# K and V loads in pairs of heads with 16 KB pieces, in a one-token decode kernel

**Chip and metric.** One core of one Trainium2 chip. The metric is the device time of the core in microseconds (us). Most executions agree within 0.3%.

**Words.** PE is the matmul engine and PEld its weight load; DVE, ACT and POOL are the vector, scalar and GpSimd engines; SP issues the loads (SPq is its queue). A *piece* is one contiguous run of bytes that a load brings to one partition. A *tick* is the count that one DMA engine adds to the load's semaphore when its share has landed: the trace holds 16 for each of these loads, with their times, though no view prints them. The *landing* of a load is its last tick.

## The reference, cut to what matters

One token `x` (512 wide) is normalised; an attention branch with 32 query heads over 8 K/V heads reads the last 4096 positions of two caches, and a gated MLP branch is added.

```python
W  = 4096                                     # min(4096, max(256, Sk // 4)), Sk = 65536
q  = (x @ wq).reshape(B, 1, 32, 128)          # wq: 512 x 4096
k, v = caches[:, :, Sk - W:, :]               # 8 heads x 4096 x 128, bf16, repeated 4 times
p  = softmax(q @ k.T * 128 ** -0.5)
a  = (p @ v).reshape(B, 1, 4096) @ wo         # wo: 4096 x 512
m  = (silu(x @ w_gate) * (x @ w_up)) @ w_down # 512 x 1792 twice, 1792 x 512
out = x_in + a + x + sigmoid(x @ w_r) * m     # x here is the normalised row
```

All weights and the used part of the caches are read once: 30.67 MB.

## The kernel before

SP issues all large loads in one order. Every load covers 128 partitions; with 16 DMA engines, each engine moves 8 partitions' pieces per load. For K and V a load is one head (1 MB), and a partition gets 32 consecutive positions, that is one piece of 8 KB.

```python
t_wq = [dma(sy, f"wq{h}", wq_sb[:, h * KH:(h + 1) * KH, :], wq_v[:, h * KH:(h + 1) * KH, :]) for h in range(2)]
t_k = [dma(sy, f"k{g}", k_sb[:, g].rearrange("p b (i d) -> p (b i) d", d=DH),
           A_k_cache[0, g, Sk - W:, :].rearrange("(p t) d -> p t d", t=NT)) for g in range(HKV)]
...                                            # then v0..v7, gate, up, wo in 4 chunks, w_down in 5
def T(b, i):                                   # 8 transposes of K on PE, into PSUM
    te.wait_ge(s_c[b], i)
    for k in range(8):
        ins = te.transpose(tp[:, b, k * P:(k + 1) * P], kin[:, b, k * P:(k + 1) * P], ident_bf[:])
    ins.then_inc(pe_t, 1)
def Sm(b, i, q, last=False):                   # 2 score matmuls, each on a column group of 32
    te.wait_ge(s_ev[b], i)
    for e in range(2):
        c = 2 * b + e
        cq, ch = c % 4, c // 4
        ins = te.matmul(sc[32 * cq:32 * cq + 32, ch, :], lhsT=q[:], rhs=kT[:, b, e * 512:(e + 1) * 512],
                        start=False, stop=False, tile_position=(0, 32 * cq), skip_group_check=True)
...
with te.Fori(1, 9) as i:                       # one head per turn, in two half steps
    T(0, i); T(1, i); te.wait_ge(s_qb, i); Sm(2, i, qB); Sm(3, i, qB, last=True)
    T(2, i); T(3, i); te.wait_ge(s_qa, i); Sm(0, i, qA); Sm(1, i, qA, last=True)
...                                            # softmax, P transposed, PV, then:
fill(F4)                                       # 2 * F4 filler matmuls
for k, (j0, j1) in enumerate(wo_chunks):       # 4 x 8 matmuls, each chunk waits for its load
    PE.need(t_wo[k]); ...
for k, (j0, j1) in enumerate(wd_chunks):       # 14 matmuls behind 5 loads
    PE.need(t_wd[k]); ...
```

Of the kernel before, what the change touches and what calls it, by code (L numbers as in the profile page):

```python
# [9 lines left out]
ALU = mybir.AluOpType  # L10
# [28 lines left out]
def kernel(  # L39
# [35 lines left out]
    W3, F1, F2, F3, F4 = 2, 2, 1, 2, 2  # L75

    sb = lambda name, shape, dt: nc.alloc_sbuf_tensor(name, shape, dt)
    k_sb = sb("k_sb", [P, HKV, 4, 1024], BF16)
    v_sb = sb("v_sb", [P, HKV, NT, DH], BF16)
    wq_sb = sb("wq_sb", [P, KT, NQ], BF16)  # L80
    kin = sb("kin", [P, 4, 1024], BF16)
    kT = sb("kT", [P, 4, 1024], BF16)
    p_sb = sb("p_sb", [P, 1024], BF16)
    vin = sb("vin", [P, 2, 16, DH], BF16)
    pTcur = sb("pTcur", [P, 8, 16], BF16)
    pvS = sb("pvS", [P, 4, DH], BF16)
    qpad = sb("qpad", [P, HKV, 32], BF16)
    qA = sb("qA", [P, 32], BF16)
    qB = sb("qB", [P, 32], BF16)
# [5 lines left out]
    ident_bf = sb("ident_bf", [P, P], BF16)  # L95
    ident_f = sb("ident_f", [P, P], F32)
# [4 lines left out]
    r32 = sb("r32", [P, 32], BF16)  # L101
    eps_t = sb("eps_t", [P, 1], F32)
# [27 lines left out]
    pT_ps = ps[:, 0, :].bitcast(BF16).rearrange("p (b c) -> p b c", c=P)  # L130
    pv_ps = ps[:, 1, :]
# [17 lines left out]
    def dma(eng, name, out_, in_):  # L149
# [9 lines left out]
    t_k = [dma(sy, f"k{g}", k_sb[:, g].rearrange("p b (i d) -> p (b i) d", d=DH),  # L159
               A_k_cache[0, g, Sk - W:, :].rearrange("(p t) d -> p t d", t=NT)) for g in range(HKV)]  # L160
# [9 lines left out]
    s_qa, s_qb = S("s_qa"), S("s_qb")  # L170
    gp.memset(qB[:], 0.0).then_inc(s_qb, 1)
# [63 lines left out]
    for hf in range(2):  # L235
# [15 lines left out]
    s_c = [S(f"s_c{b}") for b in range(4)]  # L251
# [3 lines left out]
    def pool_q(g):  # L255
        POOL.need(t_qpad[g // 4])
        if g >= 1:
            gp.wait_ge(pe_q, 2 * g)
        gp.tensor_copy(out=qA[:], in_=qpad[:, g, :]).then_inc(s_qa, 1)  # L259
        gp.wait_ge(pe_q, 2 * g + 1)  # L260
        gp.tensor_copy(out=qB[:], in_=qpad[:, g, :]).then_inc(s_qb, 1)

    def C(g, b):
        if b == 0:
            DVE.need(t_k[g])
        if g >= 1:
            DVE.need((pe_t, 4 * (g - 1) + b + 1))
        ve.tensor_copy(out=kin[:, b, :], in_=k_sb[:, g, b, :]).then_inc(s_c[b], 1)  # L268
# [82 lines left out]
    PE.need(t_nb, t_ones)
# [153 lines left out]
```

## Time and profile before

| | before |
|---|---|
| median time | 82.4 us (82.32 to 82.54) |
| profiled span | 80.7 us |
| DMA share, 10 to 50 us | 1.0 |
| rate there | 419 to 424 GB/s |
| PE, DVE, ACT busy | 75%, 54%, 37% |

Which of these counts is read in the prediction, from the chain of waits. The page's DMA section counts the packets. Nearly every packet is one piece, or one tick; the number of pieces is what the change is after:

```profile
DMA packets 4185, 30.72 MB, mean 381 GB/s; under 512 B 467, under 2 KB 598, under 8 KB 1110
```

About 3080 of the 4185 are pieces of 8 KB or more, 2048 of them K and V (16 loads of 128).

### The profile page before, as it was taken

Reading aid. Unit: us, or ns where it says so; the run is one execution under the profiler, and the core shown is the slowest. Engines: PE = TensorE matmul, PEld = TensorE weight load, DVE = VectorE, ACT = ScalarE, POOL = GpSimd, SP = SyncE. Lnnn points to the kernel's source line nnn. Section 1 sums busy time; section 2 is a strip of 40 time slices with the busy share of each in tenths; the row PEclk is TensorE's granted clock in tenths of the full one; section 3 lists DMA queues with packets and bytes.
Section 4 is the critical chain, followed back from the end, with each engine's and each line's share of the span. In section 5 each row is a group of like instructions: output and inputs, shape, how many; then the busy total and the mean of one; then the engine's idle time right before and its main releaser. Section 6 shows DMA issues by size and latency. Waiting matters only on the chain.

```text
span 80.7 us, 1552 instructions
## 1 busy us (share of the span) xinstructions
PE 60.5 (75%) x596; PEld 29.9 (37%) x596; DVE 43.5 (54%) x103; ACT 29.7 (37%) x40; POOL 7.3 (9%) x27
## 2 busy tenths in 40 slices
PE   0012945589999999999988968877888887788950
PEld 0012201386657768667732323222233322123300
DVE  3775000195678977968736678888763380000030
ACT  1941001305696896895860422442222200000000
POOL 5910000101112112121200000000000000000000
PEclk9999999555799999999999999999999999999999
DMA  1899998999999999999999999999999999999400
GB/s 33 309 439 390 455 447 374 434 418 434 418 430 410 434 410 430 414 434 406 430 410 430 406 430 414 445 447 412 426 419 413 418 426 418 416 402 398 138 2 1
DMA packets 4185, 30.72 MB, mean 381 GB/s; under 512 B 467, under 2 KB 598, under 8 KB 1110
## 3 DMA queue, kind: packets, MB, share of 16 engines
q1 hardware_dynamic: 4178, 30.67, 91.7%
q8 instruction: 2, 0.03, 0.2%
q14 instruction: 1, 0.01, 0.0%
q10 hardware_dynamic: 4, 0.00, 0.0%
HBM read 30.67 MB, written 0.00 MB: 380 GB/s over the span
## 4 chain that ended last, share of the span: by engine, by line
SPq 48%; DMA 40%; PE 6%; issue 2%; DVE 1%
SPq L151 48%; DMA k_sb<-in_A_wo_dram 40%; PE ps L467 4%; PE ps L462 2%; DVE res L471 1%; SPq L500 0%; SPq L74 0%
## 5 line engine op out<-in xcount | busy, mean ns | idle before, releaser
L276 ACT COPY kT<-ps 128x1024 bf16<-128x1024 bf16 x19 | 18.5, 1019 | 8.8 <-PE ps L302 8.7
L302 PE MATMUL ps<-ident_bf,kin 128*128 128x128 bf16 x256 | 18.7, 231 | 0.8 <-DVE kin L268 0.6
L302 PEld LDWEIGHTS ps<-ident_bf,kin 128*128 128x128 bf16 x256 | 15.8, 104 | 5.1 <-issue 4.2
L268 DVE COPY kin<-k_sb 128x1024 bf16<-128x1024 bf16 x32 | 12.2, 422 | 0.7 <-PE ps L302 0.7
L273 DVE COPY kT<-ps 128x1024 bf16<-128x1024 bf16 x13 | 9.0, 692 | 4.4 <-PE ps L302 4.3
L462 PE MATMUL ps<-k_sb,oT 128*1 128x512 bf16 x32 | 7.5, 378 | 2.0 <-DMA k_sb<-in_A_wo_dram 2.0
L394 ACT CAST pvS<-ps 128x512 bf16<-128x512 f32 x8 | 4.7, 586 | 9.6 <-PE ps L399 9.6
L471 DVE TENSOR_TENSOR res<-ps,resid 1x512 bf16<-1x512 f32 x1 | 0.7, 679 | 11.5 <-PE ps L467 11.5
L375 DVE COPY vin<-v_sb 128x2048 bf16<-128x2048 bf16 x8 | 5.5, 686 | 1.4 <-PE ps L408 1.4
L381 DVE COPY vin<-v_sb 128x2048 bf16<-128x2048 bf16 x8 | 5.5, 683 | 0.0
L408 PE MATMUL ps<-vin,pTcur 128*16 128x512 bf16 x32 | 3.1, 381 | 2.6 <-ACT pvS L394 2.2
L462 PEld LDWEIGHTS ps<-k_sb,oT 128*1 128x1 bf16 x32 | 2.4, 83 | 7.1 <-DMA k_sb<-in_A_wo_dram 3.2
L420 PE MATMUL ps<-zmov,zst 128*128 128x512 bf16 x16 | 4.7, 377 | 0.0
L228 PE MATMUL ps<-wq_sb,xnT 128*1 128x512 bf16 x32 | 2.9, 499 | 2.3 <-DMA wq_sb<-in_A_wq_dram 2.3
L310 PE MATMUL ps<-kT,qB 128*32 128x512 bf16 x36 | 4.2, 413 | 0.4 <-ACT kT L276 0.3
L244 DVE COPY qpad<-ps 128x16 bf16<-128x16 bf16 x2 | 0.3, 174 | 7.6 <-PE ps L240 7.6
L310 PE MATMUL ps<-kT,qA 128*32 128x512 bf16 x32 | 4.4, 417 | 0.0
L259 POOL COPY qA<-qpad 128x32 bf16<-128x32 bf16 x8 | 2.0, 255 | 20.6 <-DVE qpad L244 10.9
L194 PE MATMUL ps<-ident_bf,xn_row 1*128 1x1 bf16 x4 | 0.3, 165 | 4.6 <-DVE xn_row L189 4.6
L147 PE MATMUL ps<-zmov,zst 128*128 128x512 bf16 x14 | 3.7, 382 | 0.0
L234 ACT CAST q<-ps 128x512 bf16<-128x512 f32 x2 | 1.1, 589 | 6.6 <-PE ps L228 6.6
L414 PE MATMUL ps<-vin,pTcur 128*16 128x512 bf16 x32 | 3.1, 382 | 0.2 <-DVE vin L381 0.2
(85 smaller groups left out, 50.2 us busy)
## 6 DMA issues: line engine op xcount, KB each, us to landing
k_sb<-in_A_k_cache_dram SPq DMA_DIRECT2D x8, 1024.0 KB, 20.6
v_sb<-in_A_v_cache_dram SPq DMA_DIRECT2D x8, 1024.0 KB, 28.2
wq_sb<-in_A_wq_dram SPq DMA_DIRECT2D x2, 2048.0 KB, 9.5
k_sb<-in_A_wo_dram SPq DMA_DIRECT2D x4, 1024.0 KB, 32.0
wq_sb<-in_B_w_gate_dram SPq DMA_DIRECT2D x1, 1792.0 KB, 29.3
wq_sb<-in_B_w_up_dram SPq DMA_DIRECT2D x1, 1792.0 KB, 31.4
k_sb<-in_B_w_down_dram SPq DMA_DIRECT2D x2, 512.0 KB, 31.4
k_sb<-in_B_w_down_dram SPq DMA_DIRECT2D x1, 384.0 KB, 25.7
```

The costliest lines, as they stand in the source:

```text
L147: te.matmul(ps[:, 7, :], lhsT=zst[:], rhs=zmov[:], start=True, stop=True)
L151: eng.dma_start(out=out_, in_=in_).then_inc(s, 16)
L268: ve.tensor_copy(out=kin[:, b, :], in_=k_sb[:, g, b, :]).then_inc(s_c[b], 1)
L273: ve.tensor_copy(out=kT[:, b, :], in_=tp[:, b, :]).then_inc(s_ev[b], 1)
L276: ac.copy(out=kT[:, b, :], in_=tp[:, b, :]).then_inc(s_ev[b], 1)
L302: ins = te.transpose(tp[:, b, k * P:(k + 1) * P], kin[:, b, k * P:(k + 1) * P], ident_bf[:])
L310: ins = te.matmul(sc[32 * cq:32 * cq + 32, ch, :], lhsT=q[:], rhs=kT[:, b, e * 512:(e + 1) * 512], start=False, stop=False, tile_position= ...
L375: ve.tensor_copy(out=vin[:, 0], in_=v_sb[:, g, 0:16, :]).then_inc(s_va, 1)
L381: ve.tensor_copy(out=vin[:, 1], in_=v_sb[:, g, 16:32, :]).then_inc(s_vb, 1)
L394: ac.copy(out=pvS[:].rearrange("p t d -> p (t d)"), in_=pv_ps).then_inc(s_pvs, 1)
L420: te.matmul(ps[:, 7, :], lhsT=zst[:], rhs=zmov[:], start=True, stop=True)
L462: te.matmul(a_ps, lhsT=oT2[:, j:j + 1], rhs=wo_sb[:, j * D:(j + 1) * D], start=False, stop=False, skip_group_check=True)
```

## The change

Intent: fewer, larger pieces in the stream that bounds the kernel. Two heads share a load: 64 partitions per head, 64 positions each, 16 KB in one run. Partitions alternate between the two heads, so all of the compute has to follow: a permuted identity separates the heads when K is transposed, queries are padded for two halves, P is transposed in twice as many blocks, and 0/1 matrices gather the result. The first two K loads keep 8 KB pieces (half of the positions of both heads), so that work on K can begin as early as before.

```diff
-    t_k = [dma(sy, f"k{g}", k_sb[:, g].rearrange("p b (i d) -> p (b i) d", d=DH),
-               A_k_cache[0, g, Sk - W:, :].rearrange("(p t) d -> p t d", t=NT)) for g in range(HKV)]
+    def pair(name, tile_, cache, i0, i1):
+        g, n = i0 // 2, (i1 - i0) * NT
+        src = cache[0, 2 * g:2 * g + 2, Sk - W:, :].rearrange("h (q t) d -> q h t d", t=TP)
+        dst = bass.AP(tile_, i0 * NT * DH, [[HKV * NT * DH, P], [1, n * DH]])
+        t0 = (i0 % 2) * NT
+        return [dma(sy, f"{name}{i0}", dst, src[:, :, t0:t0 + n, :].rearrange("q h t d -> q h (t d)"))] * (i1 - i0)
+    t_k = sum([pair("k", k_sb, A_k_cache, a, b) for a, b in steps([0, 1, 2, 4, 6, 8])], [])
+    t_v = sum([pair("v", v_sb, A_v_cache, a, b) for a, b in steps([0, 2, 4, 6, 8])], [])
...                                            # the compute, cut:
-        ve.tensor_copy(out=kin[:, b, :], in_=k_sb[:, g, b, :]).then_inc(s_c[b], 1)
+        ve.tensor_copy(out=kin[:, 2 * h:2 * h + 2, :], in_=k_sb[:, g, 2 * h:2 * h + 2, :]).then_inc(s_c[h], 1)
-            ins = te.transpose(tp[:, b, k * P:(k + 1) * P], kin[:, b, k * P:(k + 1) * P], ident_bf[:])
+            ins = te.transpose(tp[:, b, k * P:(k + 1) * P], kin[:, b, k * P:(k + 1) * P], perm_bf[:])
+        for e in range(2):
+            for b in (b0, b0 + 1):
+                cq = (b + 2 * e) % 4
+                ins = te.matmul(sc[32 * cq:32 * cq + 32, e, :], lhsT=qAB[:, e, :],
+                                rhs=kT[:, b, :].rearrange("d (k h q) -> d h k q", h=2, q=PH)[:, e], ...)
-        for k in range(4):
-            blk = 4 * h + k
-            ins = te.transpose(pT_ps[:, blk, :], p_sb[:, blk * P:(blk + 1) * P], ident_bf[:])
+        for k in range(8):
+            ins = te.transpose(tp[:, h, k * P:(k + 1) * P], p_sb[:, h, k * P:(k + 1) * P], ident_bf[:])
...                                            # pTcur of 256 elements, collect of 8 columns, F3 2 -> 1
```

More of the change, by code (lines that the diff above doesn't have):

```diff
@@ L74 @@
     ctx.enter_context(tc.tile_critical())
-    W3, F1, F2, F3, F4 = 2, 2, 1, 2, 2
+    W3, F1, F2, F3, F4 = 2, 2, 1, 1, 2
     sb = lambda name, shape, dt: nc.alloc_sbuf_tensor(name, shape, dt)
+    HP = HKV // 2
+    PH = P // 2
     k_sb = sb("k_sb", [P, HKV, 4, 1024], BF16)
@@ L81 @@
     kin = sb("kin", [P, 4, 1024], BF16)
+    p_sb = kin[:, 0:2, :]
     kT = sb("kT", [P, 4, 1024], BF16)
-    p_sb = sb("p_sb", [P, 1024], BF16)
     vin = sb("vin", [P, 2, 16, DH], BF16)
-    pTcur = sb("pTcur", [P, 8, 16], BF16)
+    pTcur = sb("pTcur", [P, 8, 4, 2, REP], BF16)
     pvS = sb("pvS", [P, 4, DH], BF16)
-    qpad = sb("qpad", [P, HKV, 32], BF16)
-    qA = sb("qA", [P, 32], BF16)
-    qB = sb("qB", [P, 32], BF16)
+    qpad = sb("qpad", [P, HKV, 2, 32], BF16)
+    qAB = sb("qAB", [P, 2, 32], BF16)
     q4 = sb("q4", [P, 2, 512], BF16)
@@ L95 @@
     ident_bf = sb("ident_bf", [P, P], BF16)
+    perm_bf = sb("perm_bf", [P, P], BF16)
     ident_f = sb("ident_f", [P, P], F32)
@@ L101 @@
     r32 = sb("r32", [P, 32], BF16)
+    rsel = sb("rsel", [P, 4, 2, REP], BF16)
+    r16 = sb("r16", [P, 16], BF16)
     eps_t = sb("eps_t", [P, 1], F32)
@@ L113 @@
     xnT = sb("xnT", [P, KT], BF16)
+    oT_f = sb("oT_f", [P, HQ], F32)
     oT = sb("oT", [P, HQ], BF16)
@@ L116 @@
     oT2 = sb("oT2", [P, RJ], BF16)
-    pmax = sb("pmax", [P, 1], F32)
-    gm = sb("gm", [1, 32], F32)
-    nb_row = sb("nb_row", [1, 4, 32], F32)
-    nbias = sb("nbias", [P, 1], F32)
+    pmax = sb("pmax", [P, 2], F32)
+    gm = sb("gm", [2, 16], F32)
+    nb_row = sb("nb_row", [2, 8, 16], F32)
+    nbias = sb("nbias", [P, 2], F32)
     rowsum = sb("rowsum", [P, 2], F32)
-    rs1 = sb("rs1", [P, 1], F32)
     Bsel = sb("Bsel", [P, 32], F32)
@@ L129 @@
     qT_ps = ps[:, 6, 0:256].bitcast(BF16).rearrange("p (h c) -> p h c", c=P)
-    pT_ps = ps[:, 0, :].bitcast(BF16).rearrange("p (b c) -> p b c", c=P)
-    pv_ps = ps[:, 1, :]
+    pT_ps = ps[:, 0:2, :].bitcast(BF16)
+    pv_ps = ps[:, 2, :]
     a_ps = ps[0:1, 5, :]
@@ L158 @@
     t_wq = [dma(sy, f"wq{h}", wq_sb[:, h * KH:(h + 1) * KH, :], wq_v[:, h * KH:(h + 1) * KH, :]) for h in range(2)]
-    t_k = [dma(sy, f"k{g}", k_sb[:, g].rearrange("p b (i d) -> p (b i) d", d=DH),
-               A_k_cache[0, g, Sk - W:, :].rearrange("(p t) d -> p t d", t=NT)) for g in range(HKV)]
+    TP = W // PH
+    def pair(name, tile_, cache, i0, i1):
[4 more added lines that the diff above has]
+        return [dma(sy, f"{name}{i0}", dst, src[:, :, t0:t0 + n, :].rearrange("q h t d -> q h (t d)"))] * (i1 - i0)
+    steps = lambda cuts: zip(cuts[:-1], cuts[1:])
+    t_k = sum([pair("k", k_sb, A_k_cache, a, b) for a, b in steps([0, 1, 2, 4, 6, 8])], [])
     c0 = POOL.mark(gp.memset(ident_bf[:], 0.0))
@@ L169 @@
     t_kt0 = POOL.mark(gp.memset(kT[:, 2:4, :], 0.0))
-    s_qa, s_qb = S("s_qa"), S("s_qb")
-    gp.memset(qB[:], 0.0).then_inc(s_qb, 1)
+    s_q = S("s_q")
+    t_q0 = POOL.mark(gp.memset(qAB[:], 0.0))
     t_eps = DVE.mark(ve.memset(eps_t[:], EPS))
@@ L203 @@
         t_r32 = DVE.mark(ve.reduce_sum(out=r32[:], in_=ident_bf[:].rearrange("p (q j) -> p j q", q=4), axis=AX.X))
+        t_r16 = DVE.mark(ve.reduce_sum(out=r16[:], in_=ident_bf[:].rearrange("p (q j) -> p j q", q=8), axis=AX.X))
+    t_perm = DVE.mark(ve.tensor_copy(out=perm_bf[:].rearrange("p (h q) -> p h q", h=2),
+                                     in_=ident_bf[:].rearrange("p (q h) -> p h q", h=2)))
+    DVE.need(t_r32)
+    r32_v = r32[:].rearrange("p (q e r) -> p q e r", e=2, r=REP)
+    ve.tensor_copy(out=rsel[:, :, 0, :], in_=r32_v[:, :, 0, :])
+    ve.tensor_copy(out=rsel[:, 0:2, 1, :], in_=r32_v[:, 2:4, 1, :])
+    t_rsel = DVE.mark(ve.tensor_copy(out=rsel[:, 2:4, 1, :], in_=r32_v[:, 0:2, 1, :]))
     t_resid = DVE.mark(ve.tensor_tensor(out=resid[:], in0=xrow[:], in1=xn_row[:], op=ALU.add))
@@ L242 @@
         DVE.need(t_qt, t_qpad0)
-        dst = bass.AP(qpad, (4 * hf) * 32 + 16 * hf, [[HKV * 32, P], [36, 4], [1, 4]])
-        t_qpad.append(DVE.mark(ve.tensor_copy(out=dst, in_=qT_ps.rearrange("p h (c r) -> p c h r", r=32)[:, :, :, 0])))
-    t_v = [dma(sy, f"v{g}", v_sb[:, g], A_v_cache[0, g, Sk - W:, :].rearrange("(p t) d -> p t d", t=NT)) for g in range(HKV)]
+        for u in range(2):
+            dst = bass.AP(qpad, 2 * hf * 132 + 80 * u, [[HKV * 64, P], [132, 2], [32, 2], [1, 4]])
+            t_q = DVE.mark(ve.tensor_copy(out=dst, in_=qT_ps.rearrange("p h (g e r) -> p g e h r", e=2, r=32)[:, :, :, :, 0]))
+        t_qpad.append(t_q)
+    t_v = sum([pair("v", v_sb, A_v_cache, a, b) for a, b in steps([0, 2, 4, 6, 8])], [])
     SP.need(t_qp)
@@ L249 @@
     t_u = dma(sy, "u", wgu[:, KT * F:2 * KT * F], B_w_up.rearrange("(p kt) f -> p (kt f)", kt=KT))
-    s_c = [S(f"s_c{b}") for b in range(4)]
+    s_c = [S(f"s_c{h}") for h in range(2)]
     s_ev = [S(f"s_ev{b}") for b in range(4)]
@@ L256, in pool_q, with C @@
         POOL.need(t_qpad[g // 4])
-        if g >= 1:
-            gp.wait_ge(pe_q, 2 * g)
-        gp.tensor_copy(out=qA[:], in_=qpad[:, g, :]).then_inc(s_qa, 1)
-        gp.wait_ge(pe_q, 2 * g + 1)
-        gp.tensor_copy(out=qB[:], in_=qpad[:, g, :]).then_inc(s_qb, 1)
-    def C(g, b):
-        if b == 0:
+        gp.wait_ge(pe_q, g + 1)
+        gp.tensor_copy(out=qAB[:], in_=qpad[:, g]).then_inc(s_q, 1)
+    def C(g, h):
+        if h == 0:
             DVE.need(t_k[g])
         if g >= 1:
-            DVE.need((pe_t, 4 * (g - 1) + b + 1))
-        ve.tensor_copy(out=kin[:, b, :], in_=k_sb[:, g, b, :]).then_inc(s_c[b], 1)
+            DVE.need((pe_t, 4 * (g - 1) + 2 * h + 2))
+        ve.tensor_copy(out=kin[:, 2 * h:2 * h + 2, :], in_=k_sb[:, g, 2 * h:2 * h + 2, :]).then_inc(s_c[h], 1)
     def E(eng, g, b):
@@ L276, in E @@
             ac.copy(out=kT[:, b, :], in_=tp[:, b, :]).then_inc(s_ev[b], 1)
-    for b in range(4):
-        C(0, b)
+    for h in range(2):
+        C(0, h)
     for g in range(HKV):
@@ L287 @@
             C(g + 1, 0)
-            C(g + 1, 1)
         E("dve", g, 2)
@@ L291 @@
         if not last:
-            C(g + 1, 2)
-            C(g + 1, 3)
-    PE.need(t_zst, t_zmov, t_kt0)
+            C(g + 1, 1)
+    PE.need(t_zst, t_zmov, t_kt0, t_q0, t_perm)
     te.sem_inc(s_ev[2], 1)
@@ L299, in T, with Sm @@
     def T(b, i):
-        te.wait_ge(s_c[b], i)
+        if b % 2 == 0:
+            te.wait_ge(s_c[b // 2], i)
         for k in range(8):
-            ins = te.transpose(tp[:, b, k * P:(k + 1) * P], kin[:, b, k * P:(k + 1) * P], ident_bf[:])
+            ins = te.transpose(tp[:, b, k * P:(k + 1) * P], kin[:, b, k * P:(k + 1) * P], perm_bf[:])
         ins.then_inc(pe_t, 1)
-    def Sm(b, i, q, last=False):
-        te.wait_ge(s_ev[b], i)
+    def Sm(b0, i, last=False):
+        for b in (b0, b0 + 1):
+            te.wait_ge(s_ev[b], i)
         for e in range(2):
-            c = 2 * b + e
-            cq, ch = c % 4, c // 4
-            ins = te.matmul(sc[32 * cq:32 * cq + 32, ch, :], lhsT=q[:], rhs=kT[:, b, e * 512:(e + 1) * 512],
-                            start=False, stop=False, tile_position=(0, 32 * cq), skip_group_check=True)
+            for b in (b0, b0 + 1):
+                cq = (b + 2 * e) % 4
+                ins = te.matmul(sc[32 * cq:32 * cq + 32, e, :], lhsT=qAB[:, e, :],
+                                rhs=kT[:, b, :].rearrange("d (k h q) -> d h k q", h=2, q=PH)[:, e],
+                                start=False, stop=False, tile_position=(0, 32 * cq), skip_group_check=True)
         if last:
@@ L319 @@
         T(1, i)
-        te.wait_ge(s_qb, i)
-        Sm(2, i, qB)
-        Sm(3, i, qB, last=True)
+        Sm(2, i, last=True)
         T(2, i)
         T(3, i)
-        te.wait_ge(s_qa, i)
-        Sm(0, i, qA)
-        Sm(1, i, qA, last=True)
-    te.wait_ge(s_qb, 9)
-    Sm(2, 9, qB)
-    t_sc = PE.mark(Sm(3, 9, qB))
-    SP.need((s_c[3], 6))
+        te.wait_ge(s_q, i)
+        Sm(0, i)
+    t_sc = PE.mark(Sm(2, 9))
+    SP.need((s_c[1], 6))
     wo_v = A_wo.rearrange("(p j) n -> p (j n)", j=RJ)
@@ L338 @@
     t_wd = [dma(sy, f"wd{k}", wd_sb[:, j0 * D:j1 * D], wd_v[:, j0 * D:j1 * D]) for k, (j0, j1) in enumerate(wd_chunks)]
+    POOL.need((pe_t, 4 * HKV))
+    t_p0 = POOL.mark(gp.memset(p_sb, 0.0))
     DVE.need(t_sc)
-    t_pmax = DVE.mark(ve.reduce_max(out=pmax[:], in_=sc[:].rearrange("p a b -> p (a b)"), axis=AX.X))
+    t_pmax = DVE.mark(ve.reduce_max(out=pmax[:], in_=sc[:], axis=AX.X))
     fill(F1)
     PE.need(t_pmax, t_identf)
-    t_pmT = PE.mark(te.matmul(ps[0:1, 6, 0:P], lhsT=pmax[:], rhs=ident_f[:], start=True, stop=True))
+    t_pmT = PE.mark(te.matmul(ps[0:2, 6, 0:P], lhsT=pmax[:], rhs=ident_f[:], start=True, stop=True))
     DVE.need(t_pmT)
-    a = DVE.mark(ve.reduce_max(out=gm[:], in_=ps[0:1, 6, 0:P].rearrange("a (q c) -> a c q", q=4), axis=AX.X))
+    a = DVE.mark(ve.reduce_max(out=gm[:], in_=ps[0:2, 6, 0:P].rearrange("a (q c) -> a c q", q=8), axis=AX.X))
     DVE.need(a)
-    t_nb = DVE.mark(ve.tensor_scalar(out=nb_row[:], in0=gm[:].unsqueeze(1).to_broadcast([1, 4, 32]), scalar1=-SCALE, scalar2=None,
+    t_nb = DVE.mark(ve.tensor_scalar(out=nb_row[:], in0=gm[:].unsqueeze(1).to_broadcast([2, 8, 16]), scalar1=-SCALE, scalar2=None,
                                      op0=ALU.mult))
     fill(F2)
-    PE.need(t_nb, t_ones)
-    t_nbp = PE.mark(te.matmul(ps[:, 6, 128:129], lhsT=nb_row[:].rearrange("a q c -> a (q c)"), rhs=ones_f[0:1, 0:1],
+    PE.need(t_nb)
+    t_nbp = PE.mark(te.matmul(ps[:, 6, 128:130], lhsT=nb_row[:].rearrange("a q c -> a (q c)"), rhs=ident_f[0:2, 0:2],
                               start=True, stop=True))
     DVE.need(t_nbp)
-    t_nbias = DVE.mark(ve.tensor_copy(out=nbias[:], in_=ps[:, 6, 128:129]))
-    ACT.need(t_nbias)
-    t_p = [ACT.mark(ac.activation(out=p_sb[:, h * 512:(h + 1) * 512], in_=sc[:, h, :], func=ACTF.Exp, scale=SCALE, bias=nbias[:],
+    t_nbias = DVE.mark(ve.tensor_copy(out=nbias[:], in_=ps[:, 6, 128:130]))
+    ACT.need(t_nbias, t_p0)
+    t_p = [ACT.mark(ac.activation(out=p_sb[:, h, :].rearrange("p (j e) -> p e j", e=2)[:, h], in_=sc[:, h, :], func=ACTF.Exp, scale=SCALE, bias=nbias[:, h:h + 1],
                                   accum_out=rowsum[:, h:h + 1])) for h in range(2)]
-    DVE.need((s_ev[1], 8))
-    t_pv0 = DVE.mark(ve.memset(pv_ps, 0.0))
     fill(F3)
@@ L363, with stage_v @@
         PE.need(t_p[h])
-        for k in range(4):
-            blk = 4 * h + k
-            ins = te.transpose(pT_ps[:, blk, :], p_sb[:, blk * P:(blk + 1) * P], ident_bf[:])
+        for k in range(8):
+            ins = te.transpose(tp[:, h, k * P:(k + 1) * P], p_sb[:, h, k * P:(k + 1) * P], ident_bf[:])
     t_pT = PE.mark(ins)
     s_va, s_vb, s_pt, pe_pva, pe_pv, s_pvs, pe_col = S("s_va"), S("s_vb"), S("s_pt"), S("pe_pva"), S("pe_pv"), S("s_pvs"), S("pe_col")
-    def stage_v(g):
-        DVE.need(t_v[g])
-        if g >= 1:
-            DVE.need((pe_pva, g))
-        ve.tensor_copy(out=vin[:, 0], in_=v_sb[:, g, 0:16, :]).then_inc(s_va, 1)
-        DVE.need(t_pT)
-        if g >= 1:
-            DVE.need((pe_pv, g))
-        ve.tensor_copy(out=pTcur[:].rearrange("p b (q j) -> p b q j", j=REP),
-                       in_=pT_ps.rearrange("p b (q c) -> p b q c", q=4)[:, :, :, REP * g:REP * (g + 1)]).then_inc(s_pt, 1)
-        ve.tensor_copy(out=vin[:, 1], in_=v_sb[:, g, 16:32, :]).then_inc(s_vb, 1)
+    def stage_v(i):
+        g, u = i // 2, i % 2
+        DVE.need(t_v[i])
+        if i >= 1:
+            DVE.need((pe_pva, i))
+        v_in = v_sb[:, i].rearrange("p (q k) d -> p q (k d)", k=8)
+        ve.tensor_copy(out=vin[:, 0].rearrange("p (q k) d -> p q (k d)", q=4), in_=v_in[:, :, 0:4 * DH]).then_inc(s_va, 1)
+        DVE.need(t_pT)
+        if i >= 1:
+            DVE.need((pe_pv, i))
+        src = pT_ps.rearrange("p e (k q c) -> p k q e c", q=4, c=32)
+        ve.tensor_copy(out=pTcur[:], in_=src[:, :, :, :, 16 * u + REP * g:16 * u + REP * (g + 1)]).then_inc(s_pt, 1)
+        ve.tensor_copy(out=vin[:, 1].rearrange("p (q k) d -> p q (k d)", q=4), in_=v_in[:, :, 4 * DH:]).then_inc(s_vb, 1)
@@ L383 @@
     ve.memset(pvS[:], 0.0).then_inc(s_pvs, 1)
     stage_v(0)
-    DVE.need(t_p[1])
-    a = DVE.mark(ve.tensor_tensor(out=rs1[:], in0=rowsum[:, 0:1], in1=rowsum[:, 1:2], op=ALU.add))
-    DVE.need(a, t_r32)
-    t_B = DVE.mark(ve.tensor_scalar(out=Bsel[:], in0=r32[:], scalar1=rs1[:], scalar2=None, op0=ALU.mult))
+    DVE.need(t_p[1], t_r16)
+    for e in range(2):
+        t_B = DVE.mark(ve.tensor_scalar(out=Bsel[:].rearrange("p (g e r) -> p e g r", e=2, r=REP)[:, e],
+                                        in0=r16[:].rearrange("p (g r) -> p g r", r=REP), scalar1=rowsum[:, e:e + 1],
+                                        scalar2=None, op0=ALU.mult))
@@ L394 @@
         ac.copy(out=pvS[:].rearrange("p t d -> p (t d)"), in_=pv_ps).then_inc(s_pvs, 1)
-    PE.need(t_pv0)
+    PE.need(t_rsel)
     def collect(col):
         for cq in range(4):
-            ins = te.matmul(col, lhsT=pvS[:, cq, :], rhs=r32[:, REP * cq:REP * (cq + 1)], start=(cq == 0), stop=(cq == 3))
+            ins = te.matmul(col, lhsT=pvS[:, cq, :], rhs=rsel[:, cq].rearrange("p e r -> p (e r)"), start=(cq == 0), stop=(cq == 3))
         return ins
@@ L407 @@
         for tl in range(4):
-            ins = te.matmul(pv_ps[32 * tl:32 * tl + 16, :], lhsT=pTcur[:, tl, :],
+            ins = te.matmul(pv_ps[32 * tl:32 * tl + 32, :], lhsT=pTcur[:, tl].rearrange("p q e r -> p (q e r)"),
                             rhs=vin[:, 0].rearrange("p (q t) d -> p t q d", t=4)[:, tl],
@@ L413 @@
         for tl in range(4):
-            ins = te.matmul(pv_ps[32 * tl:32 * tl + 16, :], lhsT=pTcur[:, 4 + tl, :],
+            ins = te.matmul(pv_ps[32 * tl:32 * tl + 32, :], lhsT=pTcur[:, 4 + tl].rearrange("p q e r -> p (q e r)"),
                             rhs=vin[:, 1].rearrange("p (q t) d -> p t q d", t=4)[:, tl],
@@ L417 @@
         ins.then_inc(pe_pv, 1)
-        collect(psf[:, bass.ds(4 * 512 + g * REP, REP)]).then_inc(pe_col, 1)
+        collect(psf[:, bass.ds(4 * 512 + g * 8, 8)]).then_inc(pe_col, 1)
         for _ in range(W3):
@@ L421 @@
     te.wait_ge(s_pvs, 9)
-    t_col = PE.mark(collect(ps[:, 4, 4 + 28:4 + 32]))
+    t_col = PE.mark(collect(ps[:, 4, 8 + 56:8 + 64]))
     PE.need(t_B)
@@ L427 @@
     t_rden = DVE.mark(ve.reciprocal(out=rden[:], in_=ps[:, 6, 320:352]))
-    DVE.need(t_col, t_rden)
-    t_oT = DVE.mark(ve.tensor_tensor(out=oT[:], in0=ps[:, 4, 4:36], in1=rden[:], op=ALU.mult))
+    DVE.need(t_col)
+    a = DVE.mark(ve.reduce_sum(out=oT_f[:].rearrange("p (g j) -> p g j", g=HP),
+                               in_=ps[:, 4, 8:72].rearrange("p (g u j) -> p g j u", g=HP, u=2), axis=AX.X))
+    DVE.need(a, t_rden)
+    t_oT = DVE.mark(ve.tensor_tensor(out=oT[:], in0=oT_f[:], in1=rden[:], op=ALU.mult))
     DVE.need(t_oT, t_mask4)
```

## The prediction

> **What bounds the kernel now.** I read the page's chain first, then the DMA row, then the DMA view issue by issue, then the timeline of the last 20 us. The chain that ended last:
>
> ```profile
> SPq 48%; DMA 40%; PE 6%; issue 2%; DVE 1%
> SPq L151 48%; DMA k_sb<-in_A_wo_dram 40%; PE ps L467 4%; PE ps L462 2%; DVE res L471 1%; SPq L500 0%; SPq L74 0%
> ```
>
> 88% of the span is the one queue: SP issuing loads (L151) against back-pressure, then the last `wo` chunk on its way. Compute holds 7%. The loads never pause:
>
> ```profile
> 10.00:20.00 10.00, 6.76 (x61) 3.93 (x58) 3.09 (x10) 2.09 (x3) 0.42 (x2) 0.72 1.00 423
> 20.00:30.00 10.00, 9.94 (x132) 6.79 (x129) 8.00 (x19) 8.10 (x9) 1.49 (x6) 0.94 1.02 424
> 40.00:50.00 10.00, 7.98 (x68) 3.36 (x68) 6.34 (x15) 3.76 (x7) 0.21 (x1) 1.00 1.01 419
> ```
>
> (Windows view: columns are the stretch, its us, busy us of PE, weight load, DVE, ACT, POOL, granted clock, DMA share, GB/s.) The DMA share is 1.0 from 10 to 50 us, and so on to about 75 us: a stream of 30.67 MB in a fixed order (`wq`, K, V, gate, up, `wo`, `w_down`). Only a faster stream or a shorter tail can shorten the kernel. What one transfer costs, by the size of its pieces (DMA view, one issue at a time: count, KB, us from issue to landing; and the chain in time order: start, length):
>
> ```profile
> wq_sb<-in_A_wq_dram SPq DMA_DIRECT2D x1, 2048.0 KB, 7.3
> wq_sb<-in_A_wq_dram SPq DMA_DIRECT2D x1, 2048.0 KB, 11.7
> k_sb<-in_A_k_cache_dram SPq DMA_DIRECT2D x1, 1024.0 KB, 13.7
> k_sb<-in_A_k_cache_dram SPq DMA_DIRECT2D x1, 1024.0 KB, 27.5
> v_sb<-in_A_v_cache_dram SPq DMA_DIRECT2D x1, 1024.0 KB, 31.3
> ...
> 0.95 0.39 SPq L151
> 1.40 0.41 SPq L151
> 1.86 0.42 SPq L151
> 5.46 3.46 SPq L151
> 22.94 6.30 SPq L151
> ```
>
> Issue plus landing: `wq` halves at 8.25 and 13.10 us, K of head 0 at 15.56, of head 7 at 32.96, V of head 7 at 54.24. `wq` already moves in 16 KB pieces (two rows of 8 KB per partition, adjacent): 4.85 us for 2.097 MB, 432 GB/s. K has 8 KB pieces: (32.96 - 15.56) / 7 = 2.486 us for 1.049 MB, 422 GB/s. V's landings come slower, (54.24 - 32.96) / 8 = 2.66 us. The completion ticks of the 16 engines show why: fourteen keep 2.485 us per transfer, one is 0.75 us late from V of head 3 on (41.13 us against 40.39), and from head 5 on the latest is 1.5 us behind (46.95 against 45.38). Beside these stand packets of the instruction queues at 37.5 and 44.8 us. The last load landing carries this 1.4 us lag to the end (77.28 us, the other engines near 75.8).
>
> The tail (timeline: start, us, engine, line):
>
> ```profile
> 65.46 1.89 PE L462 MATMUL ps<-k_sb,oT 128*1 128x512 bf16 x8 [0.26 <-DMA k_sb<-in_A_wo_dram]
> 72.84 1.89 PE L462 MATMUL ps<-k_sb,oT 128*1 128x512 bf16 x8 [0.61 <-DMA k_sb<-in_A_wo_dram]
> 74.56 3.25 PE L467 MATMUL ps<-k_sb,hTr 128*1 128x512 bf16 x14
> 77.86 0.68 DVE L471 TENSOR_TENSOR res<-ps,resid 1x512 bf16<-1x512 f32 x1 [11.47 <-PE ps L467]
> ```
>
> The `wo` chunks come every 2.46 us and take PE 1.89: PE waits for each, but at the first only 0.26 us. Compute is thus barely ahead when `wo` begins, and could then catch up 0.6 us per chunk.
>
> **What the Trainium skill says.** (1) "DMA: Bandwidth & Descriptors", section "Where 436 GB/s comes from": the 16 ports together carry 435.2 GB/s. The 432 of the 16 KB pieces is at that ceiling, so pieces larger still would bring nothing. The trace agrees. (2) Same page, "Why small descriptors are slow (HBM only)": about 3 cycles per packet over its 32-byte beats. Estimated from that, 8 KB costs 259 cycles and two of them 518 against 515 for 16 KB: 0.6%. The trace shows more, 2 x 2.486 against 4.85, or 2.5%; I use the trace. (3) Same page, "Latency and other measured facts": rows at a pitch of a large power of two can halve the rate. The two heads of a pair lie 16 MiB apart, so this is a rival below; nothing in this trace tests it.
>
> **The change, part by part.**
> Loads: K becomes 1+1+2+2+2 heads and V 2+2+2+2. The first two K loads keep 8 KB pieces (half the keys of both heads). Seven pairs (14.7 MB) move in 16 KB pieces: 7 x (2 x 2.486 - 4.85) = 7 x 0.12 = 0.85 us. Taken from the ticks of single engines (4.87 against 4.97 us) it is 7 x 0.10 = 0.7 us. These are on the path, and everything after moves up: 0.7 to 0.85 us.
>
> Later arrival: head 2 of K now lands with head 3, near 18.0 + 4.85 = 22.9 us instead of 20.5. Its copy to `kin` began at 21.98 in the trace, but PE transposed that head only from 24.34; a copy of 2048 elements takes 0.69 (row of `vin<-v_sb`), so it is done by 23.7. Head 4 would land at 27.7, where its copy began at about 27.75. No cost.
>
> Start of K: two `qpad` copies per half instead of one, 2 x 0.17 = 0.35 us, ahead of the first `kin` copy, which is also twice as long (0.69 against 0.42): PE's first transpose 0.6 us later than 16.51. The setup ops (`perm`, `r16`, `rsel`) lengthen DVE's work around 5 to 8 us by about 1 us, in front of a `wq` half that ends at 13.1: hidden.
>
> Inner K loop: `kin` copies 32 x 422 ns become 16 x 0.69; measured in pairs the old ones took 0.76, so DVE wins 0.07 per half step. But PE sets the pace there: 16 transposes and 4 score matmuls in 1.33 us, with the four already on four column groups (four take 0.40, not 4 x 0.38). The rotation only keeps that true with the new layout. Zero. One `qAB` copy per head replaces two; it has 0.5 us of slack.
>
> Softmax and PV: 8 transposes per half of P instead of 4, of which the second half is exposed: 4 x 58 ns = 0.23 us. POOL's clearing of `p_sb` (1.8 us, as the `kT` memset of that size) begins after the last transpose and is over 2 us before the exp. `pTcur` doubles to 256 elements: DVE's small PSUM ops rise from 157 ns (1 element) to 219 (128), about 0.5 ns per element, so +0.07 us for each of 8 heads, 0.3 to 0.6 with the loop's other waits. Wider stationary and `collect` operands cost no streaming time. One more reduce for `oT_f`, 0.2 us, beside PE's gate and up matmuls. Sum on compute: 0.6 + 0.23 + 0.45 = about 1.3 us later at `wo`.
>
> Does that reach the end? PE could have started `wo` near 64.85 (there it waited 0.35 us for `up` and 0.26 for `wo`), now near 66.1. From there 46 matmuls at 0.217 us end at about 76.2. The stream's end would be 77.8 - 0.8 = 77.0. Compute stays under by some 0.8 us; the lost slack costs nothing, if my sums hold.
>
> Total: 82.4 - 0.8 = 81.6 us, 1% faster.
>
> **Rivals.** (a) Compute takes over: if the late start, PV loop and transposes cost 2.5 us rather than 1.3, PE reaches `wo` too late, and the end moves back to 81.8 to 82.5. For it: slack of only 0.26 us at the first `wo`. Against: it gains 0.6 us per chunk, and DVE is lighter in the K loop. (b) The pair layout slows the stream: adjacent partitions now alternate between heads 16 MiB apart. If that cost 5% of 35 us, the time is 83.4 or more. Against: each engine still reads whole 16 KB runs, and `wq` with 32 KB between partitions ran at full rate. (c) The lagging engine: an instruction fetch that falls elsewhere, or on another engine, moves the last landing by one unit of 0.75 us either way: 80.9 or 82.4. DVE's program gets shorter, PE's longer by 12 instructions or so after the softmax, so such a shift is quite possible. (d) Larger pieces gain more than `wq` shows: bounded by the 435 ceiling, 14.7 MB x (1/422 - 1/435) = 1.0 us.
>
> **Range and chances.** The gain of 0.7 to 1.0 us from pieces is well founded; the lag adds 0.75 us either way, compute only on the bad side. Range 80.7 to 82.5. Faster by over 2% needs 80.75, that is the pieces and one or two units of lag gone together: 0.14. Slower by over 2% needs (b), or (a) with much more than I count: 0.05. Within 2%: 0.81.
>
> **What would show it.** Right: 2 MB of K or V every 4.85 to 4.87 us, 430 GB/s or more from 20 to 52 us, gate starting about 0.8 us earlier; the chain still ending in DMA and `wo`; K's first transpose at about 17.1; `pTcur` near 290 ns; PE waiting less or not at all at the first `wo` chunk, but still at the last. Wrong: K or V at 420 GB/s or less (the piece size is not what costs), a chain that ends in PE, DVE and ACT of the PV stage (rival a), or an engine's ticks more or less than 1.4 us late at the end (rival c).

## The result

82.06 us median (82.01 to 82.21) beside 82.47 us of the kernel before: ratio 0.9954, 95% interval 0.9931 to 0.9977. Two repeats in later sets gave 0.9933 and 0.9938; the three average 0.994, a gain of 0.5 us. Ratios are the mean time of one kernel's fast runs over that of the other's of the same rounds, so not quite the ratio of the medians. The forecast had been 0.8 us.

The comparison with the reference passed, but it says little of the new layout: by an estimate from the reference's input sizes, the attention branch adds some 4e-5 to outputs of order 1, less than bf16 resolves there. A run below with K and V in the wrong layout passed it too.

The windows view of the changed kernel, for the stretches shown before and one that was not (same columns):

```profile
10.00:20.00 10.00, 6.64 (x61) 3.39 (x54) 3.10 (x8) 2.09 (x3) 0.24 (x1) 0.77 1.02 433
20.00:30.00 10.00, 9.59 (x131) 7.13 (x129) 6.83 (x11) 7.34 (x8) 1.62 (x3) 0.89 1.01 433
30.00:40.00 10.00, 9.18 (x134) 6.53 (x132) 8.03 (x13) 7.77 (x9) 1.55 (x3) 1.00 1.00 425
40.00:50.00 10.00, 7.18 (x77) 3.83 (x75) 5.35 (x13) 4.06 (x7) 2.04 (x2) 1.00 1.01 429
```

From 20 to 50 us the rate rose from between 419 and 424 GB/s to between 425 and 433, at an unchanged DMA share of 1.0. These figures are coarse, since a packet counts where it starts: from 10 to 20 us, where most of the loads are the same, they read 423 and 433. The ticks below are the measure. The page's DMA section counts the packets:

```profile
DMA packets 3177, 30.72 MB, mean 383 GB/s; under 512 B 355, under 2 KB 486, under 8 KB 998
```

1008 packets are gone: 896 are pieces (7 loads of 128), and the 112 that are missing under 512 B are 16 ticks for each of the 7 loads. The chain of waits of the changed kernel, its shares by engine and by line:

```profile
DMA 60%; PE 22%; ACT 7%; DVE 4%; SPq 2%; issue 2%
DMA k_sb<-in_A_wo_dram 46%; DMA wq_sb<-in_A_wq_dram 15%; PE ps L321 10%; ACT kT L296 6%; PE ps L489 4%; PE ps L330 3%; PE ps L484 2%; SPq L155 2%; DVE kin L288 2%; PE ps L261 1%; DVE kT L293 1%; DVE res L493 1%; PE ps L249 1%; ACT q L255 1%
```

The chain still ends in the `wo` loads. Its earlier part now runs through K's transposes (PE L321) instead of the queue, and this is easily misread as compute having become the bound. SP now gets the `wo` loads into the queue at 34.3 us without being held there, after a wait for the last K copies that they overwrite; the chain follows that wait back. The loads still wait in the queue some 30 us (they land at 64.9 to 72.3 us), and the DMA share shows no gap. So the wait costs nothing.

The tail in the timeline view of the changed kernel:

```profile
66.44 5.35 PE L484 MATMUL ps<-k_sb,oT 128*1 128x512 bf16 x24
69.90 1.38 PEld L484 LDWEIGHTS ps<-k_sb,oT 128*1 128x1 bf16 x8 [0.36 <-DMA k_sb<-in_A_wo_dram]
72.39 1.89 PE L484 MATMUL ps<-k_sb,oT 128*1 128x512 bf16 x8 [0.59 <-DMA k_sb<-in_A_wo_dram]
76.87 0.08 PEld L489 LDWEIGHTS ps<-k_sb,hTr 128*1 128x1 bf16 x1 [0.24 <-DMA k_sb<-in_B_w_down_dram]
77.39 0.68 DVE L493 TENSOR_TENSOR res<-ps,resid 1x512 bf16<-1x512 f32 x1 [9.71 <-PE ps L489]
```

PE reaches `wo` at 66.44 us, 1.0 later than before (65.46) and no longer waiting for the load. It has caught up by the third chunk, waits again for the fourth (0.59 us, before 0.61), and its very last weights wait for the last `w_down` load. The end moved from 77.86 to 77.39 us.

So the shape is as predicted and a size is wrong. The ticks of the single engines show which. This table takes the earliest of the 16 ticks of each transfer, over the K and V transfers of the size named:

| kernel, piece | transfers | us per transfer | us per 2 MB |
|---|---|---|---|
| before, 8 KB | 15 intervals of 1 MB | 2.485 | 4.970 |
| changed, 16 KB | 7 intervals of 2 MB | 4.894 | 4.894 |

A pair saves 0.076 us, not 0.10 to 0.12, and seven pairs save 0.53 us. The last landing of all came at 77.28 before; it came at 76.83, 76.74 and 76.73 us in the three profiles of the changed kernel.

### The profile page after: what moved, and what is told of

Same layout as the page of the kernel before. It is cut to its first block, busy times and chain, and to the rows that moved or that the text cites. A ratio compares the mean times of both kernels' runs of the same rounds, so it can differ in the third digit from the quotient of the medians.

```text
span 80.2 us, 1538 instructions
## 1 busy us (share of the span) xinstructions
PE 58.6 (73%) x600; PEld 30.3 (38%) x602; DVE 43.7 (54%) x94; ACT 29.9 (37%) x40; POOL 9.1 (11%) x20
## 4 chain that ended last, share of the span: by engine, by line
DMA 60%; PE 22%; ACT 7%; DVE 4%; SPq 2%; issue 2%
DMA k_sb<-in_A_wo_dram 46%; DMA wq_sb<-in_A_wq_dram 15%; PE ps L321 10%; ACT kT L296 6%; PE ps L489 4%; PE ps L330 3%; PE ps L484 2%; SPq L155 2%; DVE kin L288 2%; PE ps L261 1%; DVE kT L293 1%; DVE res L493 1%; PE ps L249 1%; ACT q L255 1%; DVE qpad L266 1%
## 5 line engine op out<-in xcount | busy, mean ns | idle before, releaser
L321 PE MATMUL ps<-perm_bf,kin 128*128 128x128 bf16 x256 | 18.9, 233 | 1.2 <-DVE kin L288 0.9
L321 PEld LDWEIGHTS ps<-perm_bf,kin 128*128 128x128 bf16 x256 | 16.0, 105 | 5.7 <-issue 4.4
L288 DVE COPY kin<-k_sb 128x2048 bf16<-128x2048 bf16 x16 | 10.9, 686 | 2.8 <-PE ps L321 1.6
L330 PE MATMUL ps<-kT,qAB 128*32 128x512 bf16 x68 | 7.2, 414 | 1.9 <-ACT kT L296 1.9
L281 POOL COPY qAB<-qpad 128x64 bf16<-128x64 bf16 x8 | 3.6, 455 | 33.2 <-PE ps L330 33.2
L427 PE MATMUL ps<-vin,pTcur 128*32 128x512 bf16 x32 | 3.2, 386 | 2.6 <-ACT pvS L412 2.2
L439 PE MATMUL ps<-zmov,zst 128*128 128x512 bf16 x16 | 4.7, 376 | 0.0
L433 PE MATMUL ps<-vin,pTcur 128*32 128x512 bf16 x32 | 3.2, 387 | 0.3 <-DVE vin L398 0.2
L330 PEld LDWEIGHTS ps<-kT,qAB 128*32 128x32 bf16 x68 | 1.9, 93 | 4.1 <-issue 1.8
L427 PEld LDWEIGHTS ps<-vin,pTcur 128*32 128x32 bf16 x32 | 1.1, 92 | 6.0 <-DVE vin L392 5.5
```

The source lines that it names most:

```text
L288: ve.tensor_copy(out=kin[:, 2 * h:2 * h + 2, :], in_=k_sb[:, g, 2 * h:2 * h + 2, :]).then_inc(s_c[h], 1)
L330: ins = te.matmul(sc[32 * cq:32 * cq + 32, e, :], lhsT=qAB[:, e, :], rhs=kT[:, b, :].rearrange("d (k h q) -> d h k q", h=2, q=PH)[:, e], s ...
L427: ins = te.matmul(pv_ps[32 * tl:32 * tl + 32, :], lhsT=pTcur[:, tl].rearrange("p q e r -> p (q e r)"), rhs=vin[:, 0].rearrange("p (q t) d ...
L439: te.matmul(ps[:, 7, :], lhsT=zst[:], rhs=zmov[:], start=True, stop=True)
```

## The experiments

All names with "a" start from the changed kernel, those with "b" from the kernel before. The theory A at the outset: the end is the stream's, and a piece costs each engine a fixed time beside its bytes. The trace before already holds three sizes to fit it: 8 pieces per engine took 1.280 us at 4 KB (`w_down`), 2.485 at 8 KB and 4.290 at 14 KB (gate and up). These lie on 0.076 us + 0.301 us per KB. For each of the 8 pieces that is 9.5 ns (the expectations below say 9.4).

**a_8k: the change without its piece size.**

```diff
-steps([0, 1, 2, 4, 6, 8])   # K
-steps([0, 2, 4, 6, 8])      # V
+steps(range(9))             # both
```

> The changed kernel with every K and V load cut back to one half of the keys of a pair: 16 loads of 1 MB in 8 KB pieces, as many and as large as in the kernel before; compute as changed; result correct. Theory A (only the stream's pieces matter; a piece costs each engine about 9.4 ns beside its bytes, so a pair saves 0.075 us and seven pairs 0.52): landings of 1 MB every 2.485 us again, time 82.5 to 82.6 us, as the kernel before. Rival B (the compute of the changed kernel, about 1.3 us later, holds part of the end): slower than the kernel before, 82.8 or more. Rival C (the gain came from the compute side or from a later fetch of instructions): stays at 82.0 to 82.1.

Measured: 82.51 us (82.4 to 82.71), ratio 0.9989 (0.9966 to 1.0012), correct. Transfers of 1 MB every 2.483 us. All of the changed compute with the old pieces takes the old time: the gain is the pieces', and the changed compute as such costs nothing that these runs can see. Rival C falls.

**b_16k and b_16k2: the loads of the change alone.** The kernel before with the changed `t_k` and `t_v`, all else as it was. The layout is wrong.

> The kernel before with nothing changed but its loads, which are those of the changed kernel (16 KB pieces, heads in pairs); the compute takes them as if they were in the old layout, so the result is wrong on purpose. Theory A: the stream alone decides, 82.0 to 82.1 us, the same as the changed kernel, pairs landing every 4.895 us on each engine. Rival B (later compute ate part of a gain of 0.8 us): 81.6 to 81.7 us here, because this compute is earlier. Rival C: 82.4 to 82.5.

> The kernel before with the changed loads again (wrong layout on purpose). Theory A: the same time as after2 within 0.1 us. Rival B (the changed kernel's compute is late enough at wo to cost something): 0.2 us or more faster than after2.

Measured: 82.0 us, ratio 0.9928 (0.9905 to 0.9952), and 82.0 us, 0.9933 (0.9911 to 0.9955) in the second set. Pairs every 4.891 and 4.893 us. The changed kernel in that second set:

> The changed kernel once more, to stand beside b_16k2 and a_f0 on one chip. Theory A (the stream's end decides; 7 pairs x 0.075 = 0.52 us): ratio to the kernel before 0.993 to 0.996, pairs every 4.895 us. If compute holds part of the end in some runs (rival B), its runs spread more widely and are slower than b_16k2's by 0.2 us or more.

Measured: 81.92 us (81.87 to 82.17), 0.9933 (0.9910 to 0.9957). It equals b_16k2: the later compute of the changed kernel takes nothing off the gain. Rival B falls.

**b_2mb: larger transfers, pieces as they were.**

```diff
+dst = bass.AP(tile_, i0 * NT * DH, [[HKV * NT * DH, P], [NT * DH, n], [1, NT * DH]])
+src = cache[0, i0:i1, Sk - W:, :].rearrange("h (p t) d -> p h (t d)", t=NT)   # n heads in one load
```

> The kernel before with loads of two heads in one transfer (2 MB for heads 2 to 7 of K and all of V, so 9 transfers for 16), the pieces still 8 KB and the layout as it was; result correct. Tells the piece from the transfer: in the trace before both scale together (8 pieces per engine and transfer). If the 9.4 ns sit on each piece: 82.4 to 82.5 us, a pair every 4.95 to 4.97 us. If they are one cost of some 75 ns per transfer and engine (its completion write): 82.0 to 82.1 us with no change of layout at all, a pair every 4.895 us.

Measured: 82.65 us, ratio 1.0004 (0.9983 to 1.0025); pairs every 4.965 us against 4.970. So it is not a cost of each transfer or of its completion: only about 0.005 of the 0.076 us could be. It sits on the piece, and the new layout was needed for the gain.

**b_4k: the suspected cost doubled.** Each head in 4 KB pieces; the order of the keys is free.

```diff
-A_k_cache[0, g, Sk - W:, :].rearrange("(p t) d -> p t d", t=NT)
+A_k_cache[0, g, Sk - W:, :].rearrange("(u p t) d -> p u (t d)", u=2, t=NT // 2)      # V alike
```

> The kernel before with each head's K and V in pieces of 4 KB (two per partition, half the keys each), still 16 loads of 1 MB; attention does not mind the order of the keys, so the result is correct. The suspected cost doubled: 8 more pieces per engine in each of 16 loads. Theory A (9.4 ns per piece): landings of 1 MB every 2.485 + 0.075 = 2.56 us, time + 1.2 us, 83.7 to 83.9 us, ratio 1.014 to 1.016. If pieces cost nothing by themselves: 82.5 to 82.6. If small pieces cost more than the line says: above 84.

Measured: 83.76 us, ratio 1.0145 (1.0121 to 1.0169), transfers mostly 2.560 us apart. The windows view of b_4k, two stretches:

```profile
20.00:30.00 10.00, 9.94 (x132) 7.38 (x130) 7.06 (x17) 7.29 (x9) 1.50 (x6) 1.00 1.02 409
30.00:40.00 10.00, 9.88 (x140) 6.94 (x138) 8.66 (x20) 7.99 (x9) 1.80 (x7) 1.00 1.03 410
```

The DMA share stays at 1.0 while the rate falls to 410: a busy share cannot tell pieces that carry more from pieces that carry less. The line gives 2.560.

**b_v32k: further along the line.** V in two loads of four heads with 32 KB pieces, layout wrong, K as in b_16k.

> As b_16k2, but V in two loads of four heads, 32 KB pieces (layout wrong on purpose). Tests the straight line through the piece sizes of the trace before: 8 pieces take 0.076 us + 0.301 us per KB of piece (4 KB 1.280, 8 KB 2.485, 14 KB 4.290; it gives 4.892 for 16 KB, measured 4.895). For 32 KB it gives 9.71 us per 4 MB, two pairs 9.79: the two V loads end 0.15 us earlier than b_16k2's four, time 0.1 to 0.2 us less. If the rate is at a ceiling already with 16 KB, 9.79 us and no change.

Measured: the V loads land 9.71 us apart, as the line says; 81.9 us, ratio 0.9921 (0.9899 to 0.9943) beside 0.9933 of b_16k2. The step in the trace is shown; 0.1 us of time is within the intervals.

**a_f4 and a_f0: how much room PE has before `wo`.**

```diff
-    W3, F1, F2, F3, F4 = 2, 2, 1, 1, 2
+    W3, F1, F2, F3, F4 = 2, 2, 1, 1, 4        # a_f4; a_f0 has 0 there
```

> The changed kernel with four more filler matmuls ahead of the wo matmuls (4 x 0.217 = 0.87 us more of PE work at that place); result correct. Theory A (PE reaches wo with slack: first wo matmul at 66.44 us, then 46 x 0.217 = 10.0 us end at 76.4, against 77.4 for the stream): the first wo matmul moves to 67.3 us, the end by less than 0.1 us, 82.0 to 82.2 us. Rival B (compute holds the end): 82.7 to 82.9 us.

Measured: 82.29 us median, but from 82.0 to 83.06, ratio 0.9966 (0.9927 to 1.0005): between the two theories. Timeline of the tail of the profiled run (82.83 us):

```profile
66.11 1.90 PE L151 MATMUL ps<-zmov,zst 128*128 128x512 bf16 x8
67.94 7.07 PE L484 MATMUL ps<-k_sb,oT 128*1 128x512 bf16 x32
74.84 3.19 PE L489 MATMUL ps<-k_sb,hTr 128*1 128x512 bf16 x14
78.07 0.68 DVE L493 TENSOR_TENSOR res<-ps,resid 1x512 bf16<-1x512 f32 x1 [9.74 <-PE ps L489]
```

All 32 `wo` matmuls run without one wait for a load, so here PE sets the end. It was already 0.6 us late before the fillers: its first K transpose came at 17.70 us against 16.97 in the changed kernel. The 16 `q` matmuls ahead of that stage show where this begins (timeline of PE, the changed kernel, then a_f4):

```profile
13.30 1.03 PE L249 MATMUL ps<-wq_sb,xnT 128*1 128x512 bf16 x16 [1.71 <-DMA wq_sb<-in_A_wq_dram]
13.31 1.88 PE L249 MATMUL ps<-wq_sb,xnT 128*1 128x512 bf16 x16 [1.81 <-DMA wq_sb<-in_A_wq_dram]
```

The fourteen profiles fall into two groups by these matmuls. In four (both kernels' first profiles, after2 and b_16k2) they took 1.03 us. There the trace has 3.4 us at full granted clock around them, then 6.8 us at half, which puts the mean clock of these runs at 0.955 to 0.958. In the other ten they took 1.87 or 1.88 us, and the K stage began 0.5 to 0.8 us later. These ten have no record of the clock before 16.6 us, and the views count that as 1.00, so their mean of 0.998 to 1.0 is not a faster PE. The six runs of a_f4 agree with this: 82.0 and 82.08 us at a mean clock of 0.956 and 0.957, 82.28 to 83.06 at 0.998 to 1.0. So with an early start the changed kernel has room for 0.9 us more work on PE, and with a late one less than that. Why PE is at full clock for the `q` matmuls in some runs only was not traced. The unaltered kernel stays clear of the limit: in that second set it took 81.95 us at a mean clock of 0.955 and 81.87 to 82.17 at 1.0.

> The changed kernel without the four filler matmuls ahead of wo (0.87 us less PE work there); result correct. Theory A: same as after2, within 0.1 us. Rival B: faster than after2 by 0.2 us or more, since PE reaches wo earlier. If PE's clock drops for want of fillers: granted clock lower after 65 us and slower.

Measured: 81.99 us, ratio 0.9936 (0.9912 to 0.996), the same as after2. Less work for PE at that place gains nothing, and without the fillers the granted clock stayed at 1.0 from 65 us on.

**a_wo and after3: a try at a better version.**

```diff
-wo_chunks = [(0, 8), (8, 16), (16, 24), (24, 32)]      # and F4 = 0
+wo_chunks = [(0, 10), (10, 20), (20, 28), (28, 32)]
```

> A try at a better version: the changed kernel without the fillers ahead of wo and with wo in chunks of 10, 10, 8 and 4 rows instead of four of 8, so that PE has 4 + 14 matmuls after the last wo chunk instead of 8 + 14 (4 x 0.217 = 0.87 us less behind that landing); as many pieces as before; result correct. If PE's chain behind the last wo landing sets the end: 0.2 us faster than after3. If the last w_down landing sets it (in after2 at 76.74 us, the last matmul's weights waiting for it): the same as after3 within 0.1 us.

> The changed kernel on the same chip, to stand beside a_wo: ratio to the kernel before 0.992 to 0.996.

Measured: a_wo 81.91 us, 0.9922 (0.9901 to 0.9944); after3 82.06 us, 0.9938 (0.9917 to 0.9959). The medians differ by 0.15 us and the intervals overlap: not settled, and small in either case, as the last `w_down` landing would have it.

**b_pad: why one engine is late.** In every other profile two of the 16 engines fall behind. One stands 0.8 to 1.3 us behind the median engine from a transfer on that lands between 41 and 44 us; another stands 1.3 to 1.7 us behind from one on that lands between 46 and 54 us, and makes the last landing. (That they are two is read from the ticks: after the second step the second-latest engine is still where the first had been.) Rival (c) of the prediction feared that this moves. b_pad moves PE's program by 60 instructions.

```diff
+            for _ in range(30):                # where PE waits for the second half of wq
+                te.matmul(ps[:, 7, 0:1], lhsT=zst[:], rhs=zmov[:, 0:1], start=True, stop=True)
```

> The kernel before with 30 one-column matmuls (60 PE instructions) added where PE waits for the second half of wq; result correct. Tests what makes one DMA engine late by some 1.5 us: theory L, PE's own instruction fetch (the 16 KB packet on the instruction queue at 44.8 us in the kernel before), which comes when PE has gone a fixed way through its program. Then that packet comes earlier by 60 instructions, well before 42 us, and one engine is late from the transfer in flight at that moment, not only from V of head 5 on; the lateness at the end is about 1.4 us as before and the time unchanged within 0.2 us. If the packet stays near 44.8 us, it is not PE's program that sets it. A second 16 KB packet would then also come well before 75 us and could make the end later by up to 0.8 us or more if it falls on the same engine.

Measured: 82.56 us, ratio 1.0005 (0.9978 to 1.0031). The DMA view of b_pad from 20 to 30 us, by queue:

```profile
q1 hardware_dynamic: 576, 4.18, 100.4%
q8 instruction: 1, 0.02, 0.7%
```

In the kernel before, the same view of that stretch has no instruction packet:

```profile
q1 hardware_dynamic: 585, 4.24, 101.8%
```

The 16 KB packet now comes at 21.2 us instead of 44.8 (the second at 69.1 instead of 75.3). In the transfer in flight then, K of head 3, one engine goes from 0.24 to 1.54 us behind the median engine, and it stays at 1.46 to 1.61 us to the end of the stream. So the packet follows PE's program: it is PE's own instruction fetch, it makes one engine late by 1.3 us, and with a stream that never pauses the lateness is not made up. The time is unchanged because the end had a lateness of this size already. The Trainium skill, "Runtime: NRT & Kernel Launch", section "Instruction fetch mechanics", says that the stream of a long program is fetched in 16 KiB blocks at a cost "mostly hidden". For PE it is here (its timeline has no wait from 20 to 25 us), for the loads beside it it is not. The other, smaller step stayed near 40 us, after an 8 KB packet of another queue at 38.4 us; it was not traced to its cause. No run took the fetch away, so its worth in time is not measured.

## Why the prediction was wrong in its size

- **What bounds the kernel**: right. The stream does before and after; undoing the pieces alone (a_8k) or doing them alone (b_16k) moves the whole difference.
- **The term "7 x 0.12", or "7 x 0.10"**: this step failed. Measured, a pair saves 0.076 us, and seven of them 0.53 us; the three ratios of the changed kernel give 0.4 to 0.6. The 8 KB side of the difference was right (2 x 2.485); the 4.85 us for 16 KB was too short by 0.044. It was taken from a single interval, between the two `wq` landings. Rounding did little harm: the latest ticks of these two loads are 4.856 us apart. But the median ticks are 4.891 apart and the earliest 4.879, and over the fourteen profiles this interval lies anywhere from 4.84 to 4.91 us, a spread over half the size of the 0.12 to be measured. The 4.87 and 0.10 from the ticks rest on the same single interval; K and V pairs took 4.894. The line through 4, 8 and 14 KB in the same trace would have given 4.892 and so 0.55 us in all.
- **"These are on the path, and everything after moves up"**: right. The last landing moved by 0.45 to 0.55 us, the end by 0.47 in the first profile.
- **Compute 1.3 us later, hidden**: right that it is hidden (a_f0, b_16k2), low in size. PE was ready for `wo` at 66.44 us, 1.6 later than the 64.85 reckoned, and the terms were off by more than their sum. Between the two profiles the K stage starts 0.45 us later (0.6 reckoned), and its last group of transposes 1.07 later (39.93, then 41.00 us), so the K loop added 0.6 where the prediction said zero; softmax and P's transposes added 0.6 (0.23 reckoned), the PV loop 0.15 (0.45 reckoned). The "No cost" for the later K pair was not quite so: the copy for head 2 waited for it from 21.95 to 23.15 us. How much of the 0.6 this wait makes was not tested. (Two small slips in the working change nothing: the `wo` chunks land every 2.49 us, not 2.46, and 66.1 + 46 x 0.217 is 76.1, not 76.2.) A missed term of the softmax: the exp, which now writes every second element of its row, took 0.83 us for each half instead of 0.68. These groups of the changed kernel show the wait, the exp and `pTcur`:

```profile
L288 DVE COPY kin<-k_sb 128x2048 bf16<-128x2048 bf16 x16 | 10.9, 686 | 2.8 <-PE ps L321 1.6 <-DMA k_sb<-in_A_k_cache_dram 1.2
L375 ACT ACTIVATE kin<-ps,nbias 128x512 bf16<-128x512 f32 x2 | 1.6, 828 | 3.5 <-DVE nbias L373 3.5
L397 DVE COPY pTcur<-ps 128x256 bf16<-128x256 bf16 x8 | 2.3, 284 | 1.6 <-PE ps L381 1.6
```

  `pTcur` at 284 ns was as predicted (290), and so were the 16 longer `kin` copies at 686 ns (0.69 us). The wider stationary operand cost 5 ns per matmul in the PV loop (386 ns, before 381), near the nothing that was predicted.
- **Rival (b), heads 16 MiB apart**: does not happen. 16 KB pieces of alternating heads lie on the line of all other loads.
- **Rival (c), the late engine**: its size varied by 0.3 us between profiles (1.36 to 1.68 at the end of V); it did not move by a unit of 0.75 us and did not go away.
- **Rival (d)**: the ceiling fits the line, whose slope of 0.301 us per KB is 435 GB/s. But 16 KB pieces are not at it, as the prediction had read from the 4.85 us: they run at 428, and 32 KB pieces at 432, so larger pieces did still bring something.

## What to carry to other kernels

When one queue of loads is busy from end to end, its busy share hides what it achieves; divide the time of many equal transfers by their number, fit a line through the piece sizes that the trace already has, and multiply the cost of a piece by the pieces that each engine is spared. A rate taken from a single interval between landings is too uncertain to measure an effect of 2% of that interval. Check how much room the other engines have before making them later, and by how much their start moves between runs. And look at whether the comparison with the reference can see the part that you changed.

## What the Trainium skill lacked or had wrong

- "DMA: Bandwidth & Descriptors", section "Why small descriptors are slow (HBM only)": the fixed cost of about 3 cycles per packet (3.5 ns at the page's 850 MHz, an estimate) is too low for these loads. From 4 to 32 KB a piece costs an engine about 9.5 ns beside its bytes; 8 to 16 KB still gains 1.5%, 4 to 8 KB 3%.
- The same page, section "Where 436 GB/s comes from": the 435.2 GB/s of the 16 ports agrees. The slope of the line, 0.301 us for 16 x 8 pieces of 1 KB, is 435 GB/s. The section's remark that the HBM side binds loads at about 358 GB/s does not hold for this one-core program, which loaded at 419 to 433 from 20 to 50 us.
- The same page, "Rules for kernel authors", counts bytes per transfer ("128 partitions, ≥1 MiB per DMA") and leaves open which size of descriptor is faster. Beyond 1 MiB, the length of the piece per partition counts: 2 MB loads with 8 KB pieces gained nothing (1.0004), with 16 KB pieces about 0.6%.
- "Runtime: NRT & Kernel Launch", section "Instruction fetch mechanics", has no word of the cost to other traffic: in b_pad one 16 KB fetch for PE left one of the 16 DMA engines 1.3 us behind for the remaining 55 us of a full stream.
